# Attention scores from hi and lo parts of Q and K in a fused attention and two-stage expert kernel

## The chip, the cores and the metric

One core of a Trainium2 chip runs the whole program. The time is in device microseconds (us) for one execution. TensorE (PE) multiplies, VectorE (DVE), ScalarE (ACT) and GpSimd (POOL) work elementwise, and SP issues most of the DMAs; POOL issues some as well. Each engine works through its own queue in order, and waits at an instruction until what it reads is there and what it writes to is free.

## The reference

Three stages follow one another. Only the first is touched, so the reference is cut to it; its result goes, as 896 rows of 768, through a gated product of two projections and then through a layer of eight experts with a router.

```python
# batch 2, 12 heads, 448 positions, head size 64, all float32
scores = scale * q @ k.T
scores = einsum('bhij,hg->bgij', scores, w_pre)      # mixes the heads
attn = exp(scores - max(scores)); attn /= sum(attn) + 1e-9
attn = einsum('bhij,hg->bgij', attn, w_post)         # mixes them again
out = attn @ v
```

## The kernel before, in words

**Blocks and iterations.** The query rows of each of the two batches are cut into four blocks of 120, 120, 120 and 90 columns (`QW`; 448 padded to 450), eight blocks in all. A block is worked through in iterations of two groups of 2 x 5 query rows: six iterations for a block of 120, five for one of 90, 46 in all (`N`), counted by n. Block starts (`first`) are n = 0, 6, 12, 18, 23, 29, 35 and 41.

**The steps.** `qk_mm` (L79 on) computes the scores of a pair of heads for one block: for each head of the pair (r, 64 partitions of Q and K) and each half of the block's columns (h) one fp32 matmul of 64 rows, up to 64 columns of weights and 448 moving columns, four per pair, each of which the profile shows as two instructions. ACT copies one head's scores from PSUM to the tile `S` of the block (L97), DVE the other's (L98). There are two tiles `S`, used by blocks in turn. `relayout` (L107) moves, for one iteration, the scores from `S` to a tile `G` whose partitions hold 5 query rows x 12 heads, by four DMAs: one on SP's queue, three on POOL's (L114). `premix` (L118) multiplies by the head weights, `rowmax` (L129, DVE) takes row maxima from PSUM, `exps` (L136, ACT) the exponentials, `norm` (L145, three small DVE steps) folds the reciprocal sums into the tile `Wp` (L153), `postmix` (L157) mixes heads again and turns the layout, `a2t` (L171) copies the result out of PSUM to `A2T`, one half on ACT, one on DVE, `av` (L181) multiplies by V, and `av_out` (L193) writes the result as a rounded part by ACT (L202) and a remainder by DVE (L203).

**The order of an iteration** (`run`, L205). The order on each engine is the order of the code. Iteration n does norm(n), postmix(n-1), the scores of at most two pairs of a later block (mostly one), premix(n+2), exps(n+1), a2t(n-1), the score copies, AV for one pair of the block before (from n = 7 on), rowmax(n+2), av_out, the re-layouts that have come due, and loads of Q, K and V on SP's queue. `AH` = 5 sets how far ahead the re-layouts run (up to that of n+5 at the end of iteration n, but never into a block whose scores aren't all done) and by when a block's scores must be done (five iterations ahead of its first). K of a batch is six tiles, one per pair, loaded for the second batch from n = 9 on. Q is one tile per block, loaded three iterations ahead of a block's second predecessor.

**After attention.** Scores of the last block are closed first, then the pools of Q, K and `S`; in their space the weights of the next stage are loaded (`Moe1.load`) and split into parts by five steps each (`split_steps`: three DVE steps of decoding, a cast on ACT, a DVE subtract). `hook` (in `build`) runs these steps behind each of the last iterations, one per iteration, and starts that stage's first matmuls behind the last.

Of the kernel before, what the change touches and what calls it, by code (L numbers as in the profile page):

```python
# [33 lines left out]
class Attention:  # L34
# [3 lines left out]
    def __init__(self, nc, tc, args, consts, xh, xl, es, psum):  # L38
        self.nc, self.tc, self.a = nc, tc, args
        self.c = consts  # L40
        self.xh, self.xl = xh, xl
        p = lambda name, bufs, **kw: es.enter_context(tc.tile_pool(name=name, bufs=bufs, **kw))
        self.qk_closed = self.s_closed = False
        self.att = p("att", 1)
        self.s_es, self.qk_es = ExitStack(), ExitStack()
        self.sp = self.s_es.enter_context(tc.tile_pool(name="scores", bufs=1))
        self.qk = self.qk_es.enter_context(tc.tile_pool(name="qk", bufs=1))
        self.ps_s, self.ps_t, self.ps_o = psum
        self.blocks = [(b, c) for b in range(B) for c in range(len(QW))]
        self.seq = []  # L50
        for blk, (b, c) in enumerate(self.blocks):
            ng = QW[c] // (2 * IG)
            for g0 in range(0, ng, 2):
                self.seq.append((blk, g0, min(2, ng - g0), g0 + 2 >= ng))
        self.Kt, self.Q, self.S = {}, {}, {}
        self.G, self.T, self.e, self.W, self.st = {}, {}, {}, {}, {}
        self.A2T, self.vt = {}, {}

    def load_k(self, b, p):
        t = self.qk.tile([128, S], F32, name="Kt", bufs=12)  # L60
        self.nc.sync.dma_start(t, self.a["kT"][b, :, p, :])
        self.Kt[b, p] = t

    def load_q(self, blk):
        b, c = self.blocks[blk]
        i0, w = QOFF[c], QW[c]
        q = self.qk.tile([128, HP, 120], F32, name="Q", bufs=2)
        src = self.a["qT"][b, :, i0 * HP:(i0 + w) * HP].rearrange("p (h i) -> p h i", h=HP)
        self.nc.sync.dma_start(q[:, :, :w], src)
        self.Q[blk] = q  # L70

    def load_v(self, b, p):
        self.vt[b, p] = self.att.tile([128, NJ, 2, D], F32, name="vt", bufs=8)[:JP]
        self.nc.sync.dma_start(self.vt[b, p], self.a["vj"][b, p])

    def qk_pair(self, blk, p, pool="s"):
# [2 lines left out]
    def qk_mm(self, blk, p, pool="s"):  # L79
# [5 lines left out]
        t = self.ps_t.tile([128, 2, 512], F32, name="t") if pool in ("ta", "tv") else None  # L85
        ps = self.pair(pool) if t is None else [t[:, 0], t[:, 1]]
        q, k = self.Q[blk], self.Kt[b, p]
        for r in range(2):
            for h, m in ((0, 64), (1, hw)):
                nc.tensor.matmul(ps[r][64 * h:64 * h + m, :S], q[64 * r:64 * r + 64, p, h * hw:h * hw + m],  # L90
                                 k[64 * r:64 * r + 64, :], start=True, stop=True)
        n = 64 + hw
        dst = self.S[blk][:n, 2 * p:2 * p + 2, :]

        def copies():
# [11 lines left out]
    def relayout(self, n):  # L107
        blk, g0, nr, last = self.seq[n]
        ng = QW[self.blocks[blk][1]] // (2 * IG)
        g = self.att.tile([128, 2, S], F32, name="G", bufs=4)  # L110
        for r in range(nr):
            for h in range(2):
                p0 = 64 * h + g0 + r
# [91 lines left out]
    def run(self, hook=None):  # L205
# [3 lines left out]
        for n, s in enumerate(self.seq):  # L209
            first.setdefault(s[0], n)  # L210
        first[nb] = N
        AH, LAG, PRE = 5, 1, 5
        c = self.c
        cs = self.att.tile([128, 4, 64], F32, name="cs")
        self.load_q(0)
        for p in range(HP):
            self.load_k(0, p)
# [29 lines left out]
        for i in range(HP):  # L247
            loads[3 + i] = lambda i=i: self.load_v(0, i)
            loads[9 + i] = lambda i=i: self.load_k(1, i)
            loads[first[len(QW)] + 1 + i] = lambda i=i: self.load_v(1, i)  # L250
        parts = []
        for n in range(N + LAG):
            av, k = [], 0
# [37 lines left out]
            if n < N:  # L291
                for tb in range(3, nb):
                    if n == first[tb - 2] - 3:
                        self.load_q(tb)
                loads.get(n, lambda: None)()
            if not todo and not self.qk_closed:
                self.qk_es.close()
                self.qk_closed = True
# [703 lines left out]
def build(nc, tc, a):  # L1002
    with ExitStack() as es0:
# [17 lines left out]
        with ExitStack() as es:  # L1021
# [4 lines left out]
            def hook(n):  # L1026
                if A.s_closed and not hasattr(m1, "wp"):
                    m1.open_w(es_x)
                if n in (N - 6, N - 4):
                    m1.load(len(m1.raw) + len(m1.hl))  # L1030
                if n in (N - 5, N - 1):
                    steps.extend(m1.split_steps(len(m1.hl)))
                if n == N:
                    fill.extend(m1.mm_steps(0, [0]))
                for q, k in ((steps, 1), (fill, 2)):
                    for f in q[:k]:
                        f()
                    del q[:k]
            A.run(hook)
            for f in fill:  # L1040
                f()
            for p in range(HP):
# [211 lines left out]
def layout(q, k, v, w_pre, w_post, moe_w_a, moe_w_b, moe_w_out, moe2_modality_id, moe2_w_gate, moe2_modality_bias,  # L1254
           moe2_w1, moe2_w2):
    C = np.ascontiguousarray
    pairs = lambda t: t.reshape(B, HP, 2, S, D).transpose(0, 2, 4, 1, 3).reshape(B, 128, HP, S)
    qt = np.pad(pairs(q), ((0, 0), (0, 0), (0, 0), (0, QCOLS - S)))
    qt = np.concatenate([qt[:, :, :, o:o + w].reshape(B, 128, -1) for o, w in zip(QOFF, QW)], axis=2)
    vj = np.zeros((B, 2, 64, NJ, H, D), np.float32)  # L1260
    vj[:, :, :JB] = v.reshape(B, H, NJ, 2, JB, D).transpose(0, 3, 4, 2, 1, 5)
    eye = np.eye(IG, dtype=np.float32)
# [1 line left out]
    for i, m in enumerate((np.tile(w_pre, (IG, IG)), np.kron(eye, np.ones((H, H), np.float32)),  # L1264
# [18 lines left out]
    sel[:, 0], sel[:, 1] = 96 + m % 32 - m, 64 + m % 64 - m  # L1283
    return {
        "kT": C(pairs(k)),
        "qT": C(qt),
        "vj": C(vj.reshape(B, 128, NJ, HP, 2, D)[:, :JP].transpose(0, 3, 1, 2, 4, 5)),
        "wmix": wmix.reshape(128, 4, 64),
        "kc": kc,
# [27 lines left out]
```

## Time and profile before

| what | value |
|---|---|
| median of 3 runs | 660.07 us (655.54 to 661.12) |
| the profiled execution | 657.97 us |
| its span, first to last instruction | 656.2 us |
| PE busy | 605.2 us (92%) |
| DVE busy | 439.0 us (67%) |
| ACT busy | 238.6 us (36%) |
| POOL busy | 137.0 us (21%) |
| mean granted TensorE clock | 0.976 |

The rows come from the one profiled execution, whose own time stands in the second line. Times in a row are from the start of the span. A busy PE is not a PE at its peak, since ends of matmuls are modelled; the starts of neighbouring steps say more. Durations on POOL are rough.

### The profile page before, as it was taken

How to read it: one execution, taken by the hardware profiler on the slowest of the kernel's cores; microseconds unless marked ns; L12 is line 12 of the kernel's file. 1: busy time of each engine (PE TensorE's matmuls, PEld its weight loads, DVE VectorE, ACT ScalarE, POOL GpSimd, SP SyncE). 2: the span in 40 equal slices, each digit the busy share in tenths (PEclk: the TensorE clock that was granted, in tenths of full speed). 3: DMA queues.
4: the chain of work that ended last, by engine and by line, in shares of the span. 5: the costliest groups of instructions: out<-in, count | busy, mean ns of one | idle time of the engine just before them, and what ended most of it. 6: DMA issues, size and time to landing. Idle time of an engine off the chain costs nothing. (4 is left out here: it accounts for less than half of the span.)

```text
span 656.2 us, 16711 instructions
## 1 busy us (share of the span) xinstructions
PE 605.2 (92%) x6839; PEld 501.7 (76%) x6839; DVE 439.0 (67%) x1020; ACT 238.6 (36%) x546; POOL 137.0 (21%) x176
## 2 busy tenths in 40 slices
PE   9788999989989999999999999999989999689790
PEld 3355666656669999999999899999987888478680
DVE  4597888868875887776766367986589434963250
ACT  4476666756652211112111163132552213632120
POOL 3544443543400000000000060000251111731010
PEclk9899999989999999999999999999999999799796
DMA  5789644843553564444531006012914811281111
GB/s 171 187 189 208 179 116 138 191 135 107 139 193 109 188 233 145 162 175 149 184 148 49 0 1 242 24 49 83 359 50 161 313 59 40 93 333 46 51 51 37
DMA packets 39106, 90.03 MB, mean 137 GB/s; under 512 B 12424, under 2 KB 17252, under 8 KB 38996
## 3 DMA queue, kind: packets, MB, share of 16 engines
q1 hardware_dynamic: 26900, 67.25, 31.1%
q0 software_dynamic: 12096, 21.35, 11.8%
q8 instruction: 65, 1.06, 0.7%
q14 instruction: 45, 0.37, 0.2%
HBM read 69.94 MB, written 5.70 MB: 115 GB/s over the span
## 5 line engine op out<-in xcount | busy, mean ns | idle before, releaser
L114 POOL DMA_DIRECT2D G<-S x132 | 76.3, 589 | 86.4 <-ACT S L97 39.9
L1113 PE MATMUL y<-ra,gh 128*128 128x384 f32 x324 | 70.8, 339 | 0.3 <-POOL ra L1089 0.3
L826 PE MATMUL ph<-ra,xsh 128*128 128x512 f32 x168 | 56.7, 420 | 11.6 <-ACT ra L789 6.5
L369 ACT CAST whi<-wdec 128x768 fp32r<-128x768 f32 x24 | 20.0, 834 | 123.8 <-DVE wdec L354 123.6
L141 ACT ACTIVATE e<-t,st 124x448 f32<-124x448 f32 x90 | 56.3, 631 | 15.9 <-DVE st L132 11.2
L167 PEld LDWEIGHTS o<-Wp,e 60*64 60x64 f32 (+1 forms) x2880 | 50.0, 134 | 15.5 <-issue 7.8
L167 PE MATMUL o<-Wp,e 60*56 60x60 f32 (+1 forms) x2880 | 57.0, 222 | 4.2 <-issue 1.7
L189 PEld LDWEIGHTS s<-A2T,vt 120*64 120x64 f32 x720 | 36.0, 138 | 32.4 <-ACT S L97 25.6
L132 DVE TENSOR_REDUCE st<-t 124x2 f32<-124x896 f32 (+1 forms) x46 | 49.2, 1070 | 13.6 <-PE t L125 13.0
L1113 PEld LDWEIGHTS y<-ra,gh 128*128 128x128 f32 x324 | 56.7, 188 | 1.2 <-POOL ra L1089 0.6
L125 PE MATMUL t<-G,wpre 60*64 60x448 f32 x360 | 51.9, 549 | 4.8 <-DMA G<-S 2.5
L1089 POOL TENSOR_TENSOR ra<-wo,ra 128x768 fp32r<-128x768 f32 x4 | 10.5, 2667 | 210.3 <-ACT ra L1088 210.3
L905 PE MATMUL py<-ra,gh 128*128 128x384 f32 x224 | 49.2, 340 | 0.0
L189 PE MATMUL s<-A2T,vt 120*64 120x120 f32 (+1 forms) x720 | 45.2, 269 | 4.3 <-ACT S L97 2.6
L90 PE MATMUL s<-Kt,Q 64*64 64x448 f32 (+2 forms) x336 | 46.9, 555 | 2.3 <-issue 1.7
L826 PEld LDWEIGHTS ph<-ra,xsh 128*128 128x128 f32 x168 | 32.9, 203 | 19.2 <-ACT ra L789 6.9
L394 PE MATMUL t<-xh,wlo 128*128 128x448 f32 x144 | 42.1, 367 | 0.5 <-DVE wlo L370 0.5
L795 POOL DMA_INDIRECT fa<-yd,idc x11 | 11.4, 1036 | 149.0 <-DVE P L718 63.4
L394 PE MATMUL t<-xl,whi 128*128 128x448 f32 x144 | 42.0, 366 | 0.0
L394 PE MATMUL t<-xh,whi 128*128 128x448 f32 x144 | 41.9, 365 | 0.0
L1113 PE MATMUL y<-ra,gl 128*128 128x384 f32 x162 | 41.2, 335 | 0.0
L905 PEld LDWEIGHTS py<-ra,gh 128*128 128x128 f32 x224 | 39.0, 188 | 0.9 <-issue 0.9
(238 smaller groups left out, 1201.0 us busy)
## 6 DMA issues: line engine op xcount, KB each, us to landing
wraw<-in_wab_dram SPq DMA_DIRECT2D x48, 384.0 KB
G<-S POOLq DMA_DIRECT2D x132, 105.0 KB, 5.9
fa<-in_w_dram SPq DMA_DIRECT2D x4, 3072.0 KB
wor<-in_w_out_dram SPq DMA_DIRECT2D x12, 768.0 KB
r1f<-in_w_dram SPq DMA_DIRECT2D x2, 3072.0 KB
G<-S SPq DMA_DIRECT2D x48, 105.0 KB
r1f<-in_wg_dram SPq DMA_DIRECT2D x8, 384.0 KB
r1f<-in_w_dram SPq DMA_DIRECT2D x4, 768.0 KB
```

Source lines behind the costliest of these rows:

```text
L90: nc.tensor.matmul(ps[r][64 * h:64 * h + m, :S], q[64 * r:64 * r + 64, p, h * hw:h * hw + m], k[64 * r:64 * r + 64, :], start=True, stop=True)
L114: (self.nc.sync if r == 0 and (h == 0 or n < 2) else self.nc.gpsimd).dma_start(g[64 * r:64 * r + GK, h, :], self.S[blk][p0:p0 + ng * (IG - ...
L125: nc.tensor.matmul(t[64 * h:64 * h + 64, r, :S], w[64 * r:64 * r + GK, :], g[64 * r:64 * r + GK, h, :], start=True, stop=True)
L132: self.nc.vector.tensor_reduce(out=st[:124, 0:nr], in_=self.T[n][:124, :nr, :S], op=ALU.max, axis=AX.X, negate=True)
L141: self.nc.scalar.activation(e[:124, r, :], t[:124, r, :S], AF.Exp, bias=st[:124, r:r + 1], scale=1.0, accum_out=st[:124, 2 + r:3 + r])
L167: nc.tensor.matmul(o[h][64 * u:64 * u + m, c0:c0 + GK], e[64 * h:64 * h + GK, r, x:x + m], wp[64 * h:64 * h + GK, r, :], start=True, stop= ...
L189: nc.tensor.matmul(ps[u * 64:(u + 1) * 64, :w], vt[:, j, u, :], at[:, j * H + 2 * p + u, :w], start=(j == 0), stop=(j == NJ - 1))
L369: lambda: nc.scalar.copy(hi, x3),
L394: self.nc.tensor.matmul(ps[hf][:, :S], w[:, d, :], x[:, d, hf * S:(hf + 1) * S], start=(d == 0 and i == 0), stop=(d == ND - 1 and i == 2))
L826: nc.tensor.matmul(ps, x[:, d], self.w1[:, hf, s, d], start=(d == 0 and i == 0), stop=(d == ND - 1 and i == 2))
L905: nc.tensor.matmul(y[q][:, :384], hx[:, f % 4], self.w2[:, f, s, q * 384:(q + 1) * 384], start=(f == 0 and i == 0), stop=(f == NFC - 1 and ...
L1113: nc.tensor.matmul(y[q][:, :384], gx[:, f % 6], wov[:, f, s, 384 * q:384 * (q + 1)], start=(t > 0 and f == 0 and i == 0), stop=(f == NF - ...
```

## The change

Blocks 2 to 7 take their scores from rounded parts. Of each K tile and of the Q tiles of these blocks a hi part is made by a copy to f32r on ACT and a lo part, the remainder, by a subtract on POOL. The scores of a pair are then hi x hi + hi x lo + lo x hi: six matmuls of 64 rows and up to 124 weight columns, where four fp32 matmuls stood. Q is laid out 128 columns wide, the second half of a block from column 64 on, and Q is loaded so. K of the first batch is split at the end of iterations 0 to 5, K of the second at 12 to 17; Q of block 2 at 0, and of blocks 3 to 7 one iteration ahead of the block two before (n = 5, 11, 17, 22, 28). The lo tiles share buffers with the raw ones. `G` has three buffers instead of four and the look-ahead `AH` is 4; V has six buffers instead of eight, and its second batch is loaded one iteration later; the mixing weights `cs` use a buffer of `G`. The score tiles are closed one iteration later; the first load of the next stage moves from N-6 to N-5 and its first split from N-5 to N-3, with two steps per iteration instead of one. Behind attention stands a drain on POOL.

```diff
     def load_k(self, b, p):
-        t = self.qk.tile([128, S], F32, name="Kt", bufs=12)
+        t = self.qk.tile([128, S], F32, name="Kt", tag="Kt", bufs=8)
...
+    def split(self, raw, hi, lo):
+        self.nc.scalar.copy(hi, raw)
+        self.nc.gpsimd.tensor_tensor(out=lo, in0=raw, in1=hi.bitcast(F32), op=ALU.subtract)
+
+    def split_k(self, b, p):
+        hi = self.qk.tile([128, S], F32R, name="Kh", bufs=6)
+        lo = self.qk.tile([128, S], F32R, name="Kl", tag="Kt", bufs=8)
+        self.split(self.Kt[b, p], hi, lo)
+        self.Kt[b, p], self.Kh[b, p] = lo, hi
+
+    def split_q(self, blk):
+        hi = self.qk.tile([128, HP, 128], F32R, name="Qh", bufs=2)
+        lo = self.qk.tile([128, HP, 128], F32R, name="Ql", tag="Q", bufs=3)
+        self.split(self.Q[blk], hi, lo)
+        self.Q[blk], self.Qh[blk] = lo, hi
...
-        q = self.qk.tile([128, HP, 120], F32, name="Q", bufs=2)
+        q = self.qk.tile([128, HP, 128], F32, name="Q", tag="Q", bufs=3)
...
-        self.vt[b, p] = self.att.tile([128, NJ, 2, D], F32, name="vt", bufs=8)[:JP]
+        self.vt[b, p] = self.att.tile([128, NJ, 2, D], F32, name="vt", bufs=6)[:JP]
...
-        for r in range(2):
-            for h, m in ((0, 64), (1, hw)):
-                nc.tensor.matmul(ps[r][64 * h:64 * h + m, :S], q[64 * r:64 * r + 64, p, h * hw:h * hw + m],
-                                 k[64 * r:64 * r + 64, :], start=True, stop=True)
         n = 64 + hw
+        if blk < 2:
+            for r in range(2):
+                for h, m in ((0, 64), (1, hw)):
+                    nc.tensor.matmul(ps[r][64 * h:64 * h + m, :S], q[64 * r:64 * r + 64, p, 64 * h:64 * h + m],
+                                     k[64 * r:64 * r + 64, :], start=True, stop=True)
+        else:
+            qh, kh = self.Qh[blk], self.Kh[b, p]
+            for i, (x, y) in enumerate(((qh, kh), (qh, k), (q, kh))):
+                for r in range(2):
+                    nc.tensor.matmul(ps[r][:n, :S], x[64 * r:64 * r + 64, p, :n], y[64 * r:64 * r + 64, :],
+                                     start=i == 0, stop=i == 2)
...
-        g = self.att.tile([128, 2, S], F32, name="G", bufs=4)
+        g = self.att.tile([128, 2, S], F32, name="G", bufs=3)
...
-        AH, LAG, PRE = 5, 1, 5
+        AH, LAG, PRE = 4, 1, 5
...
-            loads[first[len(QW)] + 1 + i] = lambda i=i: self.load_v(1, i)
+            loads[first[len(QW)] + 2 + i] = lambda i=i: self.load_v(1, i)
...
                     if n == first[tb - 2] - 3:
                         self.load_q(tb)
+                    if n == first[tb - 2] - 1:
+                        self.split_q(tb)
                 loads.get(n, lambda: None)()
+                if n == 0:
+                    self.split_q(2)
+                if n < HP:
+                    self.split_k(0, n)
+                if 0 <= n - 12 < HP:
+                    self.split_k(1, n - 12)
...
-                if n in (N - 6, N - 4):
+                if n in (N - 5, N - 4):
                     m1.load(len(m1.raw) + len(m1.hl))
-                if n in (N - 5, N - 1):
+                if n in (N - 3, N - 1):
                     steps.extend(m1.split_steps(len(m1.hl)))
...
-                for q, k in ((steps, 1), (fill, 2)):
+                for q, k in ((steps, 2), (fill, 2)):
...
             A.run(hook)
+            nc.gpsimd.drain()
```

## Rows read from the trace of the kernel before

**Rows 1.** Stages: length, busy us of each engine (instructions), clock, DMA share, GB/s.

```profile
26.60:48.40 21.80, 19.77 (x558) 13.18 (x550) 19.48 (x42) 15.66 (x41) 10.35 (x18) 0.92 0.76 189
48.40:164.50 116.10, 110.06 (x2788) 72.87 (x2788) 92.02 (x206) 74.31 (x203) 49.32 (x86) 0.99 0.59 153
```

**Rows 2.** Order of time on PE, steady: start, us, line, tile, count.

```profile
83.06 1.10 PE L167 MATMUL o<-Wp,e 60*64 60x60 f32 x62
...
84.72 1.00 PE L125 MATMUL t<-G,wpre 60*64 60x448 f32 x8
85.81 1.04 PE L189 MATMUL s<-A2T,vt 120*64 120x120 f32 x16
86.78 1.10 PE L167 MATMUL o<-Wp,e 60*64 60x60 f32 x62
87.68 0.54 PE L90 MATMUL s<-Kt,Q 64*60 64x448 f32 x1
...
88.44 1.02 PE L125 MATMUL t<-G,wpre 60*64 60x448 f32 x8
89.41 1.04 PE L189 MATMUL s<-A2T,vt 120*64 120x120 f32 x16
```

**Rows 3.** Order of time on DVE and ACT, the same stretch.

```profile
85.87 1.09 DVE L132 TENSOR_REDUCE st<-t 124x2 f32<-124x896 f32 x1 [0.18 <-PE t L125]
...
86.89 0.38 ACT L202 CAST xh<-s 128x120 fp32r<-128x120 f32 x1 [1.14 <-PE s L189]
87.06 0.63 ACT L141 ACTIVATE e<-t,st 124x448 f32<-124x448 f32 x1
...
87.99 0.28 DVE L153 TENSOR_TENSOR Wp<-wpo,st 124x120 f32<-124x120 f32 x1
...
88.78 0.62 DVE L98 COPY S<-s 124x448 f32<-124x448 f32 x1
88.81 0.55 ACT L97 COPY S<-s 124x448 f32<-124x448 f32 x1
```

**Rows 4.** Order of time on PE, an iteration without QK.

```profile
168.24 0.58 PE L125 MATMUL t<-G,wpre 60*64 60x448 f32 x2
...
169.19 1.04 PE L189 MATMUL s<-A2T,vt 120*64 120x120 f32 x16
```

**Rows 5.** First f32r matmuls of the next stage on PE; a stretch of it.

```profile
194.48 0.47 PE L394 MATMUL t<-xh,whi 128*128 128x448 f32 x1
194.78 0.37 PE L394 MATMUL t<-xl,whi 128*128 128x448 f32 x1
...
220.00:240.00 20.00, 20.00 (x101) 18.47 (x100) 16.74 (x24) 3.37 (x5) 0.00 (x0) 1.00 0.53 181
```

**Rows 6.** An ACT cast, a POOL subtract, a DVE subtract (ns min/median/max) of 768 columns.

```profile
L369 ACT CAST whi<-wdec 128x768 fp32r<-128x768 f32 x23 | 19.2, 835 | 123.6 <-DVE wdec L354 123.6
...
392.04 1.84 POOL L1089 TENSOR_TENSOR ra<-wo,ra 128x768 fp32r<-128x768 f32 x1
...
L1059 DVE TENSOR_TENSOR gl<-fa,gh x14: 947/952/2594, 361.8 to 448.3; 128x768 fp32r<-128x768 f32 x14
```

**Rows 7.** Re-layout DMAs: POOL's issues (ns, first and last start), landing of all.

```profile
L114 POOL DMA_DIRECT2D G<-S x132: 573/583/847, 12.4 to 172.5; - x132
...
DMA to landing us min/median/max: 2.7/5.9/11.5
```

**Rows 8.** Order of time on DVE, early iterations.

```profile
38.96 1.09 DVE L132 TENSOR_REDUCE st<-t 124x2 f32<-124x896 f32 x1 [0.20 <-PE t L125]
...
40.36 0.28 DVE L153 TENSOR_TENSOR Wp<-wpo,st 124x120 f32<-124x120 f32 x1
...
41.66 1.09 DVE L132 TENSOR_REDUCE st<-t 124x2 f32<-124x896 f32 x1
```

**Rows 9.** DVE, last iterations.

```profile
183.06 0.56 DVE L350 TENSOR_SCALAR wdec<-wraw 128x768 uint32<-128x768 uint32 x1 [2.03 <-DMA wraw<-in_wab_dram]
```

More of the change, by code (lines that the diff above doesn't have):

```diff
@@ L55, in __init__ @@
         self.Kt, self.Q, self.S = {}, {}, {}
+        self.Kh, self.Qh = {}, {}
         self.G, self.T, self.e, self.W, self.st = {}, {}, {}, {}, {}
@@ L59, in load_k @@
     def load_k(self, b, p):
-        t = self.qk.tile([128, S], F32, name="Kt", bufs=12)
+        t = self.qk.tile([128, S], F32, name="Kt", tag="Kt", bufs=8)
         self.nc.sync.dma_start(t, self.a["kT"][b, :, p, :])
         self.Kt[b, p] = t
+    def split(self, raw, hi, lo):
[11 more added lines that the diff above has]
+        self.Q[blk], self.Qh[blk] = lo, hi
     def load_q(self, blk):
         b, c = self.blocks[blk]
-        i0, w = QOFF[c], QW[c]
-        q = self.qk.tile([128, HP, 120], F32, name="Q", bufs=2)
-        src = self.a["qT"][b, :, i0 * HP:(i0 + w) * HP].rearrange("p (h i) -> p h i", h=HP)
-        self.nc.sync.dma_start(q[:, :, :w], src)
+        q = self.qk.tile([128, HP, 128], F32, name="Q", tag="Q", bufs=3)
+        self.nc.sync.dma_start(q, self.a["qT"][b, :, c])
         self.Q[blk] = q
     def load_v(self, b, p):
-        self.vt[b, p] = self.att.tile([128, NJ, 2, D], F32, name="vt", bufs=8)[:JP]
+        self.vt[b, p] = self.att.tile([128, NJ, 2, D], F32, name="vt", bufs=6)[:JP]
         self.nc.sync.dma_start(self.vt[b, p], self.a["vj"][b, p])
@@ L211, in run @@
         first[nb] = N
-        AH, LAG, PRE = 5, 1, 5
+        AH, LAG, PRE = 4, 1, 5
         c = self.c
-        cs = self.att.tile([128, 4, 64], F32, name="cs")
+        cs = self.att.tile([128, 2, S], F32, name="G", bufs=3)[:, 0, 0:256].rearrange("p (i j) -> p i j", i=4)
         self.load_q(0)
@@ L1257, in layout @@
     pairs = lambda t: t.reshape(B, HP, 2, S, D).transpose(0, 2, 4, 1, 3).reshape(B, 128, HP, S)
-    qt = np.pad(pairs(q), ((0, 0), (0, 0), (0, 0), (0, QCOLS - S)))
-    qt = np.concatenate([qt[:, :, :, o:o + w].reshape(B, 128, -1) for o, w in zip(QOFF, QW)], axis=2)
+    qp = np.pad(pairs(q), ((0, 0), (0, 0), (0, 0), (0, QCOLS - S)))
+    qt = np.zeros((B, 128, len(QW), HP, 128), np.float32)
+    for c, (o, w) in enumerate(zip(QOFF, QW)):
+        qt[:, :, c, :, :64] = qp[:, :, :, o:o + 64]
+        qt[:, :, c, :, 64:64 + w // 2] = qp[:, :, :, o + w // 2:o + w]
     vj = np.zeros((B, 2, 64, NJ, H, D), np.float32)
@@ L1285, in layout @@
         "kT": C(pairs(k)),
-        "qT": C(qt),
+        "qT": qt,
         "vj": C(vj.reshape(B, 128, NJ, HP, 2, D)[:, :JP].transpose(0, 3, 1, 2, 4, 5)),
```

## The prediction

> **What bounds the kernel now.** I read the stage table first: it shows where each engine is busy. Attention fills the span up to 194.5 us, where the first matmul of the next stage starts [rows 5]. What lies behind, to 656.2 us, is untouched by the diff and only starts sooner or later. So the change is worth what it does to attention's 46 iterations (n = 0 to 45, and one more to drain).
>
> Then the order of time of one steady iteration, TensorE first [rows 2]. Postmix starts at 86.78, QK at 87.68, premix at 88.44, AV at 89.41, without a gap: a PE turn of 3.6 us from one AV (85.81) to the end of premix (88.44 + 1.02 = 89.46). Then the other engines in the same stretch [rows 3]. The row maximum ends at 86.96, the exponentials start at 87.06, and ACT's copy of the scores runs from 88.81 to 89.36; AV, which takes the banks that this copy empties, starts at 89.41. So from the premix end before it (84.72 + 1.00 = 85.72) to the next possible AV there is a second turn of 3.69 us, through DVE's maximum and ACT. The two turns hand over to each other: 3.72 us from postmix to postmix (83.06 to 86.78), then 3.60 from AV to AV, 3.66 in the mean. DVE ends its copy of the scores at 88.78 + 0.62 = 89.40, just as ACT does. The reader is to see that three engines arrive together. None has more than about 0.1 us in hand, though ACT is busy only 64% of the stage and POOL 42% [rows 1].
>
> **QK in three products (36 of 48 pairs).** Now: eight instructions of 448 columns on four quarter arrays, 87.68 to 88.44, 0.76 us. After: six f32r matmuls, two row halves side by side. A full-array f32r matmul of 448 columns costs 20.00 us / 101 = 0.198 us [rows 5], so three in a row are 0.59: a gain of 0.17, if the halves overlap as the fp32 quarters do. Against it stands a price that the trace shows where the shape of the array tiles changes. Eight instructions of 448 columns take 0.76 us when a step of the same shape follows (QK, then premix) and 0.95 when AV with its 120 rows follows (premix at 168.24, AV at 169.19, no wait for data) [rows 4]: 0.19 per change. And the first f32r matmul after postmix holds 0.30 us (194.48 to 194.78), 0.10 more than later ones [rows 5]. QK now has no change of shape on either side; afterwards it has two. That makes 0.59 + 0.19 + 0.19 + 0.10 = 1.07 us at worst, 0.59 at best. I take 0.91, +0.15, since the changes beside AV are the nearest rows. The PE turn becomes 3.75, longer than the ACT turn, so an undisturbed iteration takes 3.75 instead of 3.66: 20 iterations that have QK and AV and no split, +0.1 each, are **+2 us** (36 x -0.17 = -6 to 36 x 0.31 = +11).
>
> [...]
>
> **Splits of K.** Each of 12 adds a copy of 448 columns on ACT (0.55 us, as the score copies of that size [rows 3]) and a subtract on POOL (1.84 us for 768 columns undisturbed [rows 6], so an estimated 1.1 for 448). They stand at the end of an iteration, behind the cast of AV's result and ahead of the next exponentials. Six fall in n = 12 to 17. In the pattern the cast starts at 86.89 and the exponentials at 87.06, so a copy between them pushes the ACT turn by about 0.45. The subtract starts when the copy ends, about 87.65, and lasts to about 88.75. DVE's Wp multiply, with two SBUF inputs, is due at 87.99, inside that. Later in the kernel a DVE subtract with two SBUF inputs took 2594 ns beside POOL's subtracts, against 952 as a rule [rows 6]; if Wp waits likewise, DVE is 0.75 late, and its A2T and score copies pass that on to AV. Between 0.45 and 0.75 I take 0.6: six times, **+3.6 us** (0, if the copies fit where ACT waits for AV, to 5).
>
> [...]
>
> **Splits of Q.** Six, 768 columns: 0.83 us on ACT and 1.84 on POOL [rows 6]. Four (n = 11, 17, 22, 28) stand in full iterations: exponentials 0.7 later, Wp either just ahead of POOL or up to 1.75 late. I take 0.8: **+3.2 us** (0 to 7).
>
> **Early iterations, n = 0 to 6.** There is no AV, and DVE is the tightest: its maximum starts at 38.96 and again at 41.66, 2.70 us [rows 8]. ACT has room for the copies. But Wp (40.36) starts 0.3 us after the maximum's end and meets most subtracts, for 0.6 to 1.1 us. POOL has three issues of 0.58 [rows 7] and 1.1, together 2.85 us in an iteration of about 2.9: it just holds. A third to a half of the delay reaches the loop, since it runs over two iterations and each maximum is on it once: 6 x 0.35 = **+2 us** (0 to 5).
>
> **Look-ahead four, three re-layout buffers.** Each buffer is still freed by the premix three re-layouts ahead, so no new wait is there. But a block's first re-layout can start only when its last score copy is done, now one iteration (3.66 us) nearer to its premix. From that copy's end (89.36) to premix two iterations on (88.44 + 7.32 = 95.76) there are 6.4 us. Needed: POOL's third issue, 2 x 0.58 later, and 5.9 to landing at the median: 7.1, so 0.7 late; at 2.7, the fastest, nothing is late, at 11.5, the slowest, 6.3 us [rows 7]. Until now 3.66 us of slack covered it. POOL's subtracts stand in the same queue ahead of later re-layouts, and SP's loads behind its share of them; both have about two iterations to spare. Six boundaries (blocks 2 to 7) by 0.5, since slowed iterations give time back: **+3 us** (0 to 25). [...]
>
> **The end.** DVE stands 2.03 us for the first weights of the next stage [rows 9]. Loading at N-5 and splitting at N-3, instead of N-6 and N-5, takes that wait out, and moves DVE steps of about 0.95 into the last iterations, half of which would have come behind attention anyway. **-1.4 us** (-2.5 to +1).
>
> **Nothing:** six value buffers and cs in a re-layout buffer (those loads are iterations early), wider Q loads (128 columns for 120 or 90, used three or more iterations later), and the drain: POOL's last issue starts at 172.5 [rows 7], so it has nothing left to wait for.
>
> **Sum:** 2 + 3.6 + 3.2 + 2 + 3 - 1.4 = 12.4 us. The profiled execution took 657.97 us (span 656.2 and 1.8 around it), inside the three runs (655.54 to 661.12, median 660.07): 658 + 12 = **670 us**.
>
> **Rivals.**
> 1. *TensorE alone decides, and QK gets shorter* (the other side). If no change of shape is paid, QK takes 0.59 and the PE turn 3.43. If the copies also hide while ACT waits for AV, all of 36 x 0.17 = 6 comes out, with the end 658 - 7.4 = 651; if the ACT turn keeps its 3.69, half of it, 654. For it: TensorE busy 95% of the long stage [rows 1]. Against: the second turn, of which QK is no part. It decides once QK is below 0.76 us and AV starts no later where a split stands.
> 2. *The covers hold.* QK comes out even and the splits fall into idle time: 658, give or take 4. For it: the idle shares of ACT and POOL [rows 1]. Against: three engines arrive together.
> 3. *The shorter look-ahead rules.* With landings of 9.3 us, between the median and the slowest, each boundary is 9.3 + 1.2 - 6.4 = 4 us late: 24 instead of 3, the splits hidden under it, 658 + 2 + 24 - 1.4 = 682. Against: the median.
> 4. *The row halves don't overlap.* Six times 0.198 and the changes are 1.6 us, 0.8 more, in some 26 iterations not slowed already: 670 - 2 + 21 = 689. Against: the fp32 quarters overlap.
>
> **How the numbers follow.** Chances: forecast 0.47 (own range 663 to 679), rival 1 0.13, rival 2 0.21, rival 3 0.11, rival 4 0.08. About 1%, 6.6 us, is what a measurement of this kernel can tell from no change, so "same" is 653.5 to 666.7 against the median. Faster: most of rival 1 and an edge of rival 2, 0.14. Same: the rest of both and the forecast's lower edge, 0.26. Slower: 0.60. The range 655 to 686 leaves out rival 1 and most of rival 4.
>
> **What would show it.** From QK's start to premix's: 0.91 (0.59 for rival 1, 1.6 for rival 4). After a K split, exponentials 0.45 later and Wp rows far above 0.28 us. Postmix to postmix 4.2 to 4.5 in n = 12 to 17, about 3.75 beside them. Premix waiting for G's landing at block starts, under 1 us each. I am wrong if iterations with a split are as long as their neighbours, or if the neighbours are shorter than 3.6.

## The result and the profile after

The changed kernel took 663.28 us (median of 9 runs, 662.14 to 666.86), the kernel before 659.83 us in 9 runs beside it: a ratio of 1.0078, 95% interval 1.0051 to 1.0105. It is slower: the medians lie 3.5 us apart, and the ratio makes 5.1 us of 660. Both are less than the 1% that the prediction set as its bound for "same". The forecast of 670 was 6.7 us too high; the range, 655 to 686, holds the result, but the likeliest case, slower by over 1%, did not come.

The profiled execution took 662.14 us, its span 660.4: 4.2 us more than before. The page of it, first the length, then busy us, share and count of each engine, and one DMA queue, that of TensorE's instructions:

```profile
span 660.4 us, 16690 instructions
...
PE 616.2 (93%) x6767; PEld 506.3 (77%) x6767; DVE 449.8 (68%) x1020; ACT 247.4 (37%) x564; POOL 161.6 (24%) x194
...
q8 instruction: 65, 1.06, 0.7%
```

ACT and POOL have 18 instructions more, the splits; TensorE has 72 matmuls fewer, though each pair of heads has six instead of four: an fp32 matmul stands twice in the trace, an f32r matmul once. With their weight loads, that is 144 instructions fewer ahead of the later stages, a number that will matter.

Where the 4.2 us lie is read from the order of time at four places. The next stage's first matmul starts at 206.85 instead of 194.48 [rows 5]: attention lost 12.4 us, the very sum that the prediction had for the whole. One profile's end of attention is good to some 2 us: in the kernels below, the attention of before ends between 194.2 and 199.2 us, the changed one between 205.7 and 209.3. The y stage behind it ends 13.2 us late, the last expert tile and the last small scatter 10.4, and the span 4.2. So 2.8 us came back in the expert tiles and 6.2 behind the last scatter. The prediction had left both places alone.

In attention the forecast pattern is there. Order of time on TensorE in the steady part, start, us, line, tile, count:

```profile
162.11 1.16 PE L189 MATMUL o<-Wp,e 60*64 60x60 f32 x64
163.20 0.45 PE L113 MATMUL s<-Kh,Qh 64*109 64x448 f32 x2
163.49 0.37 PE L113 MATMUL s<-Kl,Qh 64*109 64x448 f32 x2
163.70 0.36 PE L113 MATMUL s<-Kh,Ql 64*109 64x448 f32 x2
163.99 0.98 PE L147 MATMUL t<-G,wpre 60*64 60x448 f32 x8
164.90 1.04 PE L211 MATMUL s<-A2T,vt 120*64 120x120 f32 x16
165.87 1.16 PE L189 MATMUL o<-Wp,e 60*64 60x60 f32 x64
```

Each row counts two matmuls, one of each row half, and the next begins 0.21 to 0.29 us later: the halves overlap. QK to premix is 163.99 - 163.20 = 0.79 us, shorter than the 0.91 forecast; but from postmix to QK it is 1.09 us where [rows 2] have 0.90. Postmix to premix grew from 1.66 to 1.88, and the turn is 165.87 - 162.11 = 3.76, against 3.66 before and 3.75 forecast.

Order of time of ACT, POOL and DVE in an iteration with a split of K:

```profile
88.70 0.37 ACT L224 CAST xh<-s 128x120 fp32r<-128x120 f32 x1 [1.56 <-PE s L211]
88.86 0.58 ACT L66 CAST Kh<-Kt 128x448 fp32r<-128x448 f32 x1
89.35 0.63 ACT L163 ACTIVATE e<-t,st 124x448 f32<-124x448 f32 x1
...
90.57 0.65 ACT L201 COPY A2T<-o 120x480 f32<-120x480 f32 x1
...
89.78 1.03 DVE L175 TENSOR_TENSOR Wp<-wpo,st 124x120 f32<-124x120 f32 x1
...
89.53 1.15 POOL L67 TENSOR_TENSOR Kl<-Kt,Kh 128x448 fp32r<-128x448 f32 x1 [2.70 <-ACT Kh L66]
```

The exponentials start 0.65 us behind the cast of AV's result, where [rows 3] have 0.17, and Wp takes 1.03 us instead of 0.28 beside POOL's subtract. An iteration like this lasts 4.08 us from copy to copy (90.57 to 94.65). Both signs that the prediction named are there; which of them costs the time is for the experiments.

### The profile page after: what moved, and what is told of

Read it like the earlier page. It is cut to its first block, busy times and chain, and to the rows that moved or that the text cites. A ratio compares the mean times of both kernels' runs of the same rounds, so it can differ in the third digit from the quotient of the medians.

```text
span 660.4 us, 16690 instructions
## 1 busy us (share of the span) xinstructions
PE 616.2 (93%) x6767; PEld 506.3 (77%) x6767; DVE 449.8 (68%) x1020; ACT 247.4 (37%) x564; POOL 161.6 (24%) x194
## 3 DMA queue, kind: packets, MB, share of 16 engines
q0 software_dynamic: 12096, 21.35, 11.4%
q8 instruction: 65, 1.06, 0.7%
## 5 line engine op out<-in xcount | busy, mean ns | idle before, releaser
L856 PE MATMUL ph<-ra,xsh 128*128 128x512 f32 x168 | 55.2, 410 | 9.1 <-ACT ysb L991 6.7
L189 PEld LDWEIGHTS o<-Wp,e 60*56 60x56 f32 (+1 forms) x2880 | 48.1, 133 | 19.0 <-DVE A2T L201 9.8
L147 PE MATMUL t<-G,wpre 60*64 60x448 f32 x360 | 57.8, 574 | 4.6 <-DMA G<-S 4.6
L189 PE MATMUL o<-Wp,e 60*56 60x60 f32 (+1 forms) x2880 | 54.6, 221 | 7.2 <-DVE A2T L201 5.2
L856 PEld LDWEIGHTS ph<-ra,xsh 128*128 128x128 f32 x168 | 32.2, 198 | 15.9 <-ACT ysb L991 7.1
L400 DVE TENSOR_TENSOR wlo<-wdec,whi 128x768 fp32r<-128x768 f32 x24 | 23.0, 958 | 21.5 <-ACT whi L399 21.5
```

The lines of the kernel that those rows point to most:

```text
L147: nc.tensor.matmul(t[64 * h:64 * h + 64, r, :S], w[64 * r:64 * r + GK, :], g[64 * r:64 * r + GK, h, :], start=True, stop=True)
L189: nc.tensor.matmul(o[h][64 * u:64 * u + m, c0:c0 + GK], e[64 * h:64 * h + GK, r, x:x + m], wp[64 * h:64 * h + GK, r, :], start=True, stop= ...
L400: lambda: V.tensor_tensor(out=lo, in0=x3, in1=hi.bitcast(F32), op=ALU.subtract)]
L856: nc.tensor.matmul(ps, x[:, d], self.w1[:, hf, s, d], start=(d == 0 and i == 0), stop=(d == ND - 1 and i == 2))
```

## The experiments

All times are medians, the ratio is to the kernel before run on the same chip. The next columns are from each profile: the start of the next stage; three tile changes in the expert stage (from the start of a tile's output copy on ACT until ACT comes to the wait for the next tile's; of the tiles that the stage works through, the third to the fourth, the sixth to the seventh and the seventh to the eighth); from the last small scatter to the end of the span; and the length of POOL's closing drain, a record of the trace that the page doesn't count as busy.

| kernel | us | ratio (95%) | next stage | tile changes | scatter to end | closing drain |
|---|---|---|---|---|---|---|
| before | 659.83 | 1 | 194.5 | 13.0, 12.1, 17.7 | 14.8 | 6.69 |
| changed | 663.28 | 1.0078 (1.0051 to 1.0105) | 206.9 | 11.4, 15.4, 11.3 | 8.6 | 1.70 |
| 1 changed, no drain | 666.88 | 1.0141 (1.0103 to 1.0180) | 205.7 | 11.4, 16.9, 11.3 | 13.3 | 6.69 |
| 2 before, drain alone | 654.86 | 0.9940 (0.9906 to 0.9974) | 199.2 | 13.5, 11.6, 16.1 | 8.7 | 1.69 |
| 3 before, shifted code | 654.33 | 0.9963 (0.9933 to 0.9992) | 194.2 | 11.4, 13.9, 11.3 | 15.9 | 6.69 |
| 4 changed, TensorE's code put back | 667.02 | 1.0146 (1.0105 to 1.0187) | 209.3 | 13.1, 11.3, 16.5 | 8.7 | 1.70 |
| 5 look-ahead alone | 665.30 | 1.0109 (1.0042 to 1.0176) | 199.6 | 13.1, 11.6, 16.0 | 15.8 | 6.76 |
| 6 changed, fp32 scores | 663.51 | 1.0080 (1.0041 to 1.0119) | 207.7 | 13.1, 11.3, 16.3 | 8.6 | 1.70 |
| 7 changed, no subtract | 716.86 | 1.0871 (1.0790 to 1.0953) | 205.5 | other tiles | | 1.93 |
| 8 products, two splits | 664.47 | 1.0070 (1.0034 to 1.0106) | 200.6 | 11.4, 18.1, 11.3 | 9.7 | 1.76 |
| 9 before, drain and shift | 648.43 | 0.9843 (0.9798 to 0.9889) | 195.4 | 11.4, 14.1, 11.3 | 8.5 | 1.69 |
| 10 the same, larger shift | 657.59 | 0.9977 (0.9947 to 1.0008) | 195.0 | 13.5, 16.8, 14.6 | 8.7 | 1.69 |
| 11 before, two drains | 654.32 | 0.9920 (0.9892 to 0.9948) | 196.2 | 15.4, 11.6, 17.4 | 8.8 | 1.69 |
| 12 before, relayouts on SP | 684.75 | 1.0409 (1.0328 to 1.0491) | 225.7 | 13.1, 11.3, 16.1 | 9.4 | 1.71 |

Theory at the start: the prediction's attention is right, and what came back behind it hangs either on the drain, or on where TensorE's code lies, or on when weights and tiles arrive.

**1. Without the drain.**

```diff
             A.run(hook)
-            nc.gpsimd.drain()
```

> The changed kernel without the drain on POOL. If the drain costs nothing by itself (POOL's wait at that place has TensorE's work as cover, as the prediction had it), attention ends where it ends in the changed kernel, 12.4 us behind the kernel before, the expert tiles follow as there, and the time is within 1 us of the changed kernel's 663.3. If the drain holds POOL's later work back (the relayouts are over, but the first code of the next stages stands behind it), the part behind attention becomes shorter and the time falls to 660 or below. If the expert part depends only on how many instructions stand ahead of it on each engine, one instruction fewer on POOL may move a stall at a tile change: the offsets of the tiles then differ by 1 to 3 us with attention unchanged.

**2. The drain alone, in the kernel before.**

```diff
             A.run(hook)
+            nc.gpsimd.drain()
```

> The kernel before with the drain as its only edit. No cost: 659.8 within 1 us, and attention's end at 194.5 us of the span as before. If the drain is what shortened the part behind attention in the changed kernel (there it took 8 to 9 us less than before), the tail behind the last scatter falls from 13.8 to about 8 us and the time to about 652.

Measured: the drain is worth more than either expectation allows in kernel 1, and kernel 2 comes out between its two cases. Order of time at the very end: of the kernel before, the last row and the span,

```profile
core 0 of [0], span 656.2 us
...
641.36 1.01 POOL L963 DMA_INDIRECT out_dram<-ysb,idx  x1 [1.52 <-DVE ysb L962]
```

of the changed kernel,

```profile
core 0 of [0], span 660.4 us
...
651.78 1.01 POOL L993 DMA_INDIRECT out_dram<-ysb,idx  x1 [1.61 <-DVE ysb L992]
```

of the changed kernel without the drain,

```profile
core 0 of [0], span 663.9 us
...
650.65 1.01 POOL L993 DMA_INDIRECT out_dram<-ysb,idx  x1 [1.52 <-DVE ysb L992]
```

and of the kernel before with it:

```profile
core 0 of [0], span 655.3 us
...
646.64 1.01 POOL L963 DMA_INDIRECT out_dram<-ysb,idx  x1 [1.52 <-DVE ysb L962]
```

From the last row to the end there are 14.8 and 13.3 us without the drain, 8.6 and 8.7 with it. No engine computes there, so the timeline shows nothing; the reader has to subtract. What fills it stands in the records of POOL's control instructions (start, us):

```
before      646.64 1.81 INC_SWDGE_SEM   648.65 6.69 DRAIN
changed     656.14 0.60 INC_SWDGE_SEM   656.94 1.70 DRAIN   (and behind attention 186.89 5.66 DRAIN)
no drain    654.39 1.81 INC_SWDGE_SEM   656.40 6.69 DRAIN
drain alone 651.99 0.60 INC_SWDGE_SEM   652.78 1.69 DRAIN   (and behind attention 175.12 6.45 DRAIN)
```

Every kernel has a drain on POOL at its end. A drain behind attention takes 5.7 to 7.0 us where POOL has nothing else to do, and the closing one, which nothing covers, is 5.0 us shorter, with 1.2 us off the step before it. What else differs between the closes is the time from the last scatter to that step, 3.7 to 6.3 us. The gain in the medians is 1.0141 to 1.0078, 4 us, in the changed kernel, and 0.6% alone. That of kernel 2 is less than its close shows, because attention ended 4.75 us late in its profile. Nearly half of that is a pause of TensorE at 196.7, without a data wait:

```profile
198.82 0.48 PE L167 MATMUL o<-Wp,e 60*56 60x60 f32 x6 [2.09 <-issue]
```

A block of TensorE's instructions begins to arrive at 196.45, as at the tile changes of the next experiment. Kernel 11, which ends attention 1.7 us late, has such a pause of 2.43 us at 193.5, with a block from 193.61. Kernels 9 and 10, with the same drain, have none there and are 1.0 and 0.5 late. So it is not the drain by itself; why the pause comes in some kernels and not in others is open.

**3. The kernel before with shifted code**, and **4. the changed kernel with TensorE's count put back.** Both only add small operations in the prologue; the first also 18 copies and 19 memsets of one column on ACT and POOL.

```diff
         self.exps(0)
+        d2 = self.ps_o.tile([128, 512], F32, name="o")
+        for i in range(56):    # 72 in the other
+            nc.tensor.matmul(d2[0:8, 0:8], z[:, 0:8], z[:, 0:8], start=True, stop=True)
```

> The kernel before, plus small operations that compute nothing, in idle time of the first 25 us: 56 matmuls of 8 columns on TensorE (112 instructions with their weight loads, so that the code behind attention stands 112 later, which is the 144 fewer of the changed kernel when counted in steps of 256), 18 copies of one column on ACT and 19 memsets of one column on POOL (the number that the splits and the drain put ahead there). Theory of the code's place: the time behind attention depends on where the branches of the expert part lie in the engines' instruction streams; then this kernel has the changed kernel's expert part, that is the tail behind the last scatter falls from 13.8 to 7.6 us and the tiles lose some 3 us, and the time is about 651 to 653, with attention as before (its end within 1.5 us of 194.5). Theory of the timing: the 8 to 9 us come from when the tiles' data and weights arrive relative to attention; then the tail stays at 13.8 us and the time at 659 to 661.

> The changed kernel, plus 72 matmuls of 8 columns on TensorE in idle time of the first 25 us, so that TensorE's code behind attention stands where it stood before the change (the count of 144 is restored); ACT's and POOL's counts stay those of the changed kernel. If TensorE's place in its code is what shortened the expert part, the 8 to 9 us come back: attention's end stays at 206.9, and the time is 670 to 672. If it is ACT's or POOL's place, or the timing, the time stays at 663 within 1.5 us.

Measured: the first and the third tile change follow the place of TensorE's code in every kernel; the second does so with a wide spread. The three are 11.4, 13.9 to 18.1 and 11.3 us in all five kernels whose code lies 144 instructions earlier or 112 later (changed, 1, 3, 8, 9). They are 13.0 to 15.4, 11.3 to 12.1 and 16.0 to 17.7 in all seven that have the count of the kernel before (before, 2, 4, 5, 6, 11, 12). Kernel 3 was expected to have the short close as well: that was wrong, its closing drain is 6.69, since this part was the drain's. For the same reason kernel 4 gives back only the tiles' part: from the last copy of the y stage to the last small scatter it takes 170.6 us, the changed kernel 167.4, the kernel before 170.2. Its 667.0 stays under the 670 to 672 expected, and it ends attention 2.4 us later than the changed kernel; at iteration 0, behind the padding, it stood 3.4 us later.

What such a change looks like: the kernel before, order of time on TensorE at the third of them.

```profile
607.99 0.51 PE L905 MATMUL py<-ra,gl 128*128 128x384 f32 x2
611.93 1.19 PE L826 MATMUL ph<-ra,xsh 128*128 128x512 f32 x2 [3.43 <-issue]
612.92 0.63 PE L826 MATMUL ph<-ra,xsl 128*128 128x512 f32 x1
613.35 1.05 PE L826 MATMUL ph<-ra,xsh 128*128 128x512 f32 x2
```

Its busy time, then granted clock, DMA share and GB/s, in the gap and behind it:

```profile
608.00:611.90 3.90, 0.50 (x3) 0.88 0.32 122
611.90:618.00 6.10, 6.07 (x15) 0.52 0.10 40
```

The queue of TensorE's instructions from 608.7 to 611.9, packets, MB and share:

```profile
q8 instruction: 1, 0.02, 1.9%
```

The changed kernel at the same change:

```profile
624.70 0.51 PE L935 MATMUL py<-ra,gl 128*128 128x384 f32 x2
625.05 0.63 PE L856 MATMUL ph<-ra,xsh 128*128 128x512 f32 x2
625.51 0.40 PE L856 MATMUL ph<-ra,xsl 128*128 128x512 f32 x1
625.75 0.62 PE L856 MATMUL ph<-ra,xsh 128*128 128x512 f32 x2
```

And kernel 4, with the 144 instructions put back:

```profile
628.24 1.19 PE L859 MATMUL ph<-ra,xsh 128*128 128x512 f32 x2 [3.45 <-issue]
```

TensorE stands 3.43 us, waits for no data, and one block of its instructions arrives meanwhile. Then the granted clock is 0.52 for the next 6.1 us, and two matmuls take 1.05 us instead of 0.62. The stand of 3.4 and half of the slow 6.1 are the 6.4 us between 17.7 and 11.3. In the changed kernel the next tile's first matmul follows without a gap; it pays at the second change instead, 15.4 for 12.1. Over the three changes together the five shifted kernels take 38.4 us in the mean (36.6 to 40.8), six of the others 41.1 (40.6 to 42.8; kernel 11, at 44.5, left out): 2.8 us, with ranges that touch. The whole stretch from the y stage's last copy to the last small scatter parts them: 166.1 to 167.7 us in the changed kernel and kernels 1, 3 and 9, and 168.8 to 173.6 in the seven with the count of before (kernel 8 is left out; it gets other tokens, see below).

How much code a block holds, and that q8 brings TensorE's, is read from the pace behind attention, in packets of 16 KB: in the kernel before 11 of them come from 226.9 to 491.2 us, while TensorE runs 1404 matmuls and 1403 weight loads, 255 instructions for a block; in the changed kernel 11 from 225.8 to 495.3 us, beside 1422 and 1420, 258 for a block. The two shifts, -144 and +112, differ by 256 instructions, about one such block, and have one pattern; the gap has a block's packet in it. How the place of the code makes TensorE stand is not shown.

**5. The look-ahead alone**, in the kernel before.

```diff
-        g = self.att.tile([128, 2, S], F32, name="G", bufs=4)
+        g = self.att.tile([128, 2, S], F32, name="G", bufs=3)
-        AH, LAG, PRE = 5, 1, 5
+        AH, LAG, PRE = 4, 1, 5
```

(and the hook's lines as in the change)

> The kernel before with the shorter look-ahead alone: relayouts issued 4 iterations ahead instead of 5, three buffers for them instead of four, and the next stage's loads and split steps moved in the hook as in the change. The prediction's term: waits of the premix for its relayout, 3 us, less 1.4 at the end of attention, so attention ends 1 to 3 us later than before (194.5), at 196 to 197. Rival: the relayouts land in time with three buffers too; attention then ends within 1 us of the kernel before or earlier, and the 12.4 us that attention lost in the changed kernel lie in the splits and products.

**6. The scores in fp32, from the hi parts.**

```diff
-        if blk < 2:
+        if blk >= 2:
+            q, k = self.Qh[blk].bitcast(F32), self.Kh[b, p].bitcast(F32)
+        if True:
```

> The changed kernel with the six blocks' scores computed as before, four quarter-array fp32 matmuls for each pair of heads; they read the hi parts alone, so the lo parts enter no score. All splits, buffers and the drain stay. TensorE's count of instructions is that of the kernel before. The prediction's term for the products is 2 us of attention's 12.4: attention's end moves from 206.9 to about 205, and the turn of an iteration between splits from 3.76 to 3.66 us. Rival: the products, with the change of TensorE's tile shape around them, cost most of it: attention's end at 200 or below. Expert part: by the theory of the code's place it has no gain here (offsets as at attention's end, within 2 us), while the closing drain stays short.

**7. Without the subtractions.**

```diff
     def split(self, raw, hi):
         self.nc.scalar.copy(hi, raw)
-        self.nc.gpsimd.tensor_tensor(out=lo, in0=raw, in1=hi.bitcast(F32), op=ALU.subtract)
```

> The changed kernel without the 18 subtractions on POOL: the hi part stands in for the lo part in the products, so the scores are other numbers; the 18 casts on ACT stay, and the products. If the subtractions (1.1 us for K, 1.9 for Q, beside which a 0.28-us product on DVE was seen to take 1.0) are the price of the splits, the iterations with K splits fall from 4.08 to 3.8 us and attention's end from 206.9 to 201 to 203. If it is the casts in ACT's chain (0.57 and 0.84 us ahead of the exponentials), attention's end stays above 205.

**8. The products with two splits.**

```diff
-            qh, kh = self.Qh[blk], self.Kh[b, p]
+            (qh, q), (kh, k) = self.qparts, self.kparts
...
-                    if n == first[tb - 2] - 1:
-                        self.split_q(tb)
...
-                if n < HP:
-                    self.split_k(0, n)
-                if 0 <= n - 12 < HP:
-                    self.split_k(1, n - 12)
+                if n == 0:
+                    self.split_k(0, 0)
```

> The changed kernel with one split of one K pair and one of one Q block at the start, whose parts serve in all products: the other blocks' K and Q are loaded but not used in blocks 2 to 7, so the scores there are other numbers. Products, look-ahead, loads and drain stay; 16 of 18 splits are gone. By the prediction's terms 6.8 us of the splits' steady part and about 1.5 of the early iterations go: attention's end at 198 to 199. Rival: the products and the shorter look-ahead carry the loss: it stays at 203 or above.

Measured, by the start of the next stage: look-ahead alone +5.1 us, more than expected; products on top of it +6.1, between the two cases, so about 1.0 for the products; the whole +12.4, so 6.3 for the splits. Some of these ends hold pauses like that of kernel 2, so the iterations are the better measure, each taken at the start of ACT's copy to `A2T`. From iteration 0 to 41 the changed kernel and kernels 1 and 4, with the same attention, fall behind the kernel before by 12.1, 11.9 and 12.2 us; kernel 5 by 4.6, kernel 8 by 6.6, kernel 7 by 8.8. That gives 4.6 for the look-ahead, 2.1 for the products and 5.4 for the splits. The kernels with the attention of before (2, 3, 9, 10, 11) move by -3.3 to +1.5 on the same count, so each part is known to 2 or 3 us.

Kernel 6 ends 0.8 later than the changed kernel instead of 2 earlier, after a loss of 3.6 us in iteration 31, part of it a 1.57-us wait for a relayout; at iteration 28, ahead of it, the two stand within 0.03 us (144.18 and 144.15). By iteration 28 the products cost between nothing and 1.8 us (kernels 5 and 8: 138.46 and 140.23). The cleanest count is from iteration 32 to 36, where nothing pauses: the kernels with the products (changed, 7, 8) lose 0.36 to 0.37 us to the kernel before, kernels 5 and 6 between -0.05 and 0.05. That is 0.09 us for an iteration.

Kernels 7 and 8 have other scores and so send other tokens to the experts. Kernel 8's last tile works on 64 columns of the array where the kernel before has 32, and takes 5.3 us longer; so of these two kernels' times only attention is read.

TensorE's waits from 26 to 210 us for the landing of a relayout, total, times, longest: in kernel 5,

```profile
PE t L125 <- DMA G<-S: 4.1, 6, 1.4
```

and in the changed kernel:

```profile
PE t L147 <- DMA G<-S: 3.3, 5, 1.3
```

The kernel before has no such line in the same stretch. The attention of kernel 5 falls back by 2.1 to 2.3 us at each of iterations 5, 11, 14, 21 and 43, and takes 1.6 to 2.1 back at 8, 13, 29 and 42.

In kernel 7 the split iterations, order of time on ACT and DVE:

```profile
86.58 0.58 ACT L66 CAST Kh<-Kt 128x448 fp32r<-128x448 f32 x1
87.07 0.63 ACT L160 ACTIVATE e<-t,st 124x448 f32<-124x448 f32 x1
...
88.29 0.65 ACT L198 COPY A2T<-o 120x480 f32<-120x480 f32 x1
...
92.37 0.64 ACT L198 COPY A2T<-o 120x480 f32<-120x480 f32 x1
...
87.50 0.28 DVE L172 TENSOR_TENSOR Wp<-wpo,st 124x120 f32<-124x120 f32 x1
```

Wp is back at 0.28 us, and yet this iteration is 92.37 - 88.29 = 4.08 us, like the one with the subtractions above. From iteration 12 to 17 the changed kernel falls back by 3.0 us, kernel 7 by 2.45, kernel 8, which has no split there, by 0.5. So it is mainly the cast ahead of the exponentials that costs there, 2.0 of the 2.5 us; what Wp loses mostly hides behind the exponentials.

In the early iterations it is the other way round. From 0 to 6 the changed kernel falls back by 4.5 us, kernel 8 by 2.6, and kernel 7, which has all the casts, by 2.4: there the subtractions cost about 2 us. The expectation of 201 to 203 without the subtractions was missed by the end of attention, 205.5, but that end includes a pause of 1.85 us at 200.0, again without a data wait and with a block of TensorE's instructions from 199.5. From iteration 0 to 41 kernel 7 loses 3.2 us less than the changed kernel. So neither case of the expectation is shown: both parts of a split cost, at different places.

The expert part of kernels 5 and 6 came as the theory of the code's place had it, even where the expectation spoke only of the time; so did the three tile changes of kernel 8.

**9 and 10. Drain and shift together, in the kernel before**: the edits of 2 and of 3 without ACT's and POOL's part, with 56 and with 92 matmuls.

> The kernel before with two additions: the drain on POOL behind attention, and 56 matmuls of 8 columns on TensorE in idle time of the first 25 us (no padding on ACT or POOL). If the two gains seen apart add up (5 to 6 us at the close from the drain; 4.4 us in the expert tiles from the place of TensorE's code, with the padding on TensorE alone enough), the closing drain takes 1.7 us, the last small scatter comes 3 to 5 us earlier than in the kernel before against attention's end, and the median is 648 to 651, some 8 us under the kernel before. If ACT's or POOL's place matters too, only the drain's part is there: 652 to 655.

> As the run beside it, but with 92 matmuls of 8 columns (184 instructions with their weight loads). If the gain in the expert tiles hangs on where the code lies in steps of 256 instructions, the stalls at the tile changes differ again from both the kernel before and the one with 56, by 1 to 6 us at single tile changes, in either direction; attention's end moves by under 2 us. If any shift gave the gain, the tiles are those of the run beside it.

Measured: kernel 9 takes 648.43 us, 0.9843 of the kernel before, as expected, and faster than both kernels. The padding on TensorE alone does it. The larger shift gives a third pattern, 13.5, 16.8 and 14.6, whose sum is 44.9. From the y stage's last copy to the last small scatter kernel 10 loses 2.8 us to the kernel before, of the 6.2 that the close gains. So it is not any shift, and the 2.8 us that the changed kernel gains are a matter of luck in where the code falls.

**11. Two drains.**

```diff
+            if n == 20:
+                nc.gpsimd.drain()
             if hook:
                 hook(n)
```

> The kernel before with two drains on POOL, one after iteration 20 of attention, when about 75 of its 132 relayout transfers are issued, and one behind attention. If a drain's length goes with the transfers that POOL issued since the last one (closing drain 6.69 us after 152, 1.70 us after 20: 0.038 us each and 0.94 us), they take about 3.8 and 3.1 us and the closing one 1.7. If its length is fixed, or goes with POOL's time since the start, the first takes 5.7 us or more, or the second stays at 5.7 to 6.5. Attention: POOL can issue no relayout during the first, so up to 4 us may be lost there; the gain at the close is that of the single drain.

Measured: POOL's records show 10.41 us from 99.30, 6.99 us from 171.74, behind attention, and 1.69 at the close. The proportion to the transfers gave 3.8 and 3.1 for the first two, so it fell as it stood. But it took no account of transfers under way: the last ones issued ahead of the two drains land at 106.6 and 176.3 us. Past these landings the drains take 3.1 and 2.4 us, after some 75 and 57 transfers, and those behind attention in kernel 2 and the changed kernel 2.6 each, after 132. So these four covered drains last until the last landing and 2.4 to 3.1 us more, whatever the number. The closing 6.69 us of the kernel before, with all relayouts long landed, don't follow from that. Attention lost nothing to the first drain: its offset to the kernel before is 1.07 us at iteration 18 and 1.06 at 26, so a POOL held for 10 us is covered by a look-ahead of five.

**12. All relayouts on SP.**

```diff
-                (self.nc.sync if r == 0 and (h == 0 or n < 2) else self.nc.gpsimd).dma_start(
+                self.nc.sync.dma_start(
```

> The kernel before, without any drain added, with all relayouts issued by SP, so that POOL issues only the expert part's 20 indirect transfers. If the relayouts that POOL issues are what the long closing drain clears away, it takes 1.7 us here, and the end behind the last small scatter takes about 9 us instead of 14.8. If any first drain on POOL late in the kernel takes 6 us or more, it stays at 6.7. Attention: SP has 180 relayouts of about 0.58 us to issue, some 2.3 us for an iteration of 3.66 us, with the weight loads behind them, so its end moves by 0 to 6 us; TensorE's code stays where it was.

Measured: the closing drain takes 1.71 us without any drain before it. So the long one is left by the relayouts that POOL issues, though the last of them landed some 470 us before it. Attention pays 31 us for it, far over the 6 expected, so this is no way to get the gain.

## Why the prediction was right in attention and wrong in the sum

The step that failed is its first: "What lies behind, to 656.2 us, is untouched by the diff and only starts sooner or later", with the drain under "nothing". The diff touches that part twice. The drain costs nothing that the runs show where it stands, as forecast (though not for the reason given: it waits 3 to 5 us for the last relayouts to land, and TensorE's work covers it). But it takes 6.2 us from the close; the prediction asked what the drain waits for, not what a later drain would be spared. And 144 instructions fewer on TensorE move the code of the expert tiles: 2.8 us in this profile. 12.4 + 0.9 (between the two stages) - 2.8 - 6.2 gives, but for rounding, the 4.2 us of the spans. With these two terms the forecast would have been about 661. That the stated range held is therefore in part luck: its middle left out 9 us of gain. Rival 2, which had 658 give or take 4, was close in time but not in cause, since attention lost what it said would hide.

In attention the sum of 12.4 came out to the tenth, which is luck too: the errors cancel, and one profile's end is good to some 2 us.

- *Products, +2.* Measured 0 to 2.1, and 0.09 an iteration where nothing pauses, for the 0.1 forecast. The turn of 3.76 is right. QK takes 0.79 up to premix, and 0.19 more stand ahead of it: 0.98 in all, between the 0.91 taken and the worst case of 1.07. Rivals 1 and 4 fall with that.
- *K splits, +3.6 for n = 12 to 17.* Measured 2.5, by kernels 8 and the changed one. The exponentials' delay carries 2.0 of it, 0.3 each; that Wp is held up was rightly foreseen (1.03 us beside the subtract, 0.28 without), and counted too high: taking the subtractions away (kernel 7) gave back 0.6.
- *Early iterations, +2.* Measured 1.9 by kernel 8 and 2.0 by kernel 7: here the subtractions are the price, as the prediction had it.
- *Splits of Q, +3.2 for four.* From iteration 18 to 28, with two of them, the changed kernel loses 3.6 us and kernel 8 2.7: 0.9 for the two, where the prediction had 1.6.
- *All splits, 8.8.* Measured 5.4 from iteration 0 to 41, 6.3 by the end of attention.
- *Look-ahead and the end, +3 and -1.4.* Kernel 5 has both: +5.1, not 1.6; 4.4 of it are there at iteration 41. The waits for G are as forecast in kind, at block starts, but up to 1.4 us instead of under 1; they add up to 4.1, far from the 24 of rival 3. The end lost instead of gaining (0.7 us behind iteration 41 in kernel 5, 2.3 in the changed kernel, 0.2 in kernel 1), as order of time on TensorE and DVE in the changed kernel shows:

```profile
201.10 0.29 PE L189 MATMUL o<-Wp,e 60*64 60x60 f32 x2 [1.49 <-DVE Wp L175]
...
204.00 1.87 PE L211 MATMUL s<-A2T,vt 120*64 120x120 f32 x16
...
198.80 0.56 DVE L380 TENSOR_SCALAR wdec<-wraw 128x768 uint32<-128x768 uint32 x1 [0.41 <-DMA bb<-in_bias_dram]
199.39 0.96 DVE L382 SCALAR_TENSOR_TENSOR wdec<-wraw,wdec 128x768 uint32<-128x768 uint32 x1
```

Two stretches there, busy time of the engines, then the granted clock, DMA share and GB/s:

```profile
195.00:200.00 5.00, 4.61 (x117) 3.47 (x112) 3.34 (x8) 3.27 (x9) 0.00 (x0) 1.00 0.91 300
200.00:207.00 7.00, 5.28 (x113) 4.46 (x113) 4.40 (x13) 1.91 (x5) 0.00 (x0) 0.63 0.41 131
```

Two steps of the next stage's weights, one of them after a wait, stand on DVE ahead of Wp. Postmix waits 1.49 us, the granted clock falls to 0.63, and AV takes 1.87 us instead of 1.04. The wait for weights of [rows 9] did not go; it moved to where the last iterations pay for it.

Open are what exactly POOL's drain clears and why the closing one takes 6.69 us without one before it, and why TensorE pauses, with a block of its instructions under way, in the last iterations of some kernels and not of others.

## What to carry to other kernels

Subtract the last instruction from the end of the span: a close of 14 us with no engine busy is a term like any other, and where POOL had issued 132 re-layouts, a drain on it in a covered place bought part of it (6 us of the close here, 4 in the medians). An edit far ahead can change how long TensorE stands at later tiles: with 144 instructions fewer on TensorE the third tile change took 11.3 us instead of 17.7, the second 15.4 instead of 12.1. So compare the tile changes one by one before a few microseconds are put down to the edit, and test it with padding of the same length. A cast on ACT, busy 66% of the time from 52 to 175 us in the changed kernel, still cost 2.0 us in six iterations, put straight ahead of the work that the loop waits for.

## What was not expected of the hardware

POOL's closing drain keeps a price for transfers that landed some 470 us before: 6.69 us with POOL's 132 relayouts, 1.71 without them, 1.70 after another drain. A drain in the middle of attention took 10.41 us, 7.3 of them until the last transfer had landed, and cost attention nothing. Between two tiles TensorE stood 3.43 us without a wait for data, while a block of its instructions arrived, and the granted clock of 0.52 for 6.1 us behind it cost about as much again.
